# Cosine-weighted linear attention and a Swish MLP on one core: transposes by DMA and attention matmuls in 64-wide array tiles

## The chip, the core and the metric

The kernel runs on one core of a Trainium2 chip. The metric is the device time in microseconds of one execution. Beside it stand the span of a profiled execution (from its first to its last instruction) and the clock that TensorE was granted, as a share of the full clock.

## What is computed

Eight batches, eight heads, 576 positions, 64 features per head. In the attention, q and k pass a relu and are weighted by the cosine and the sine of their position, which doubles the features to 128; v is summed against k once per head, and every query reads that sum. The rows are then fed to an MLP of width 512 to 2048 to 512 with g = h * sigmoid(beta h).

```python
q_p = phi(q, cos_w, sin_w)          # relu(q)*cos, relu(q)*sin
k_p = phi(k, cos_w, sin_w)
kv = np.einsum('bhsf,bhsd->bhfd', k_p, v)
z = np.sum(k_p, axis=2)
num = np.einsum('bhsf,bhfd->bhsd', q_p, kv)
den = np.einsum('bhsf,bhf->bhs', q_p, z)[..., None] + 1e-06
attn_out = num / den
x = attn_out.transpose(0, 2, 1, 3).reshape(B * S, H * D)     # 4608 x 512
h = x @ w_in
g = h * (1.0 / (1.0 + np.exp(-beta * h)))
return g @ w_out
```

## The kernel before

**Layout.** A batch's position is 9p + n, with p from 0 to 63 and n from 0 to 8. `raw_q`, `raw_k` and `raw_v` hold a batch in fp32: partition (g, p) with g the parity of the head, then four head pairs' members j, then n and the features. So one partition half holds the even heads and the other the odd ones.

**Attention of a batch.** `q_relu` and `k_relu` write `qb` and `rk` in bf16. `v_scale` writes v times the cosine and times the sine into `vb`, whose 65th column holds the weight itself, so that one product gives the sum over k too. `q_transpose` turns q on TensorE, 18 blocks of 128x128 in three groups u, and takes each group out of PSUM twice: `rt_c` is a copy, `rt_s` a product with the tangent (since sin = cos * tan, the common cosine falls out in the division and only meets the epsilon, in `epsc`). `kv_mm` is, for each half jp of the heads, 18 matmuls of 64x128 weights and 260 moving columns; `kv_mask` multiplies them by a block mask into `kv`, because 128 weight columns hold two heads and only the diagonal blocks are wanted. `num(b, ci)` takes 128 positions (64 in the last of five groups): 8 matmuls of 128x128 weights and 130 columns, then `den`, `rden` and `x_sb`. `x_transpose` turns the four 128x128 blocks of `x_sb` on TensorE and copies them to `xt`.

**MLP.** The 4608 rows go in nine chunks c of 512. A chunk has 32 slots: slots 0 to 15 are `h_group(c, jt)`, four matmuls of 512 columns into one of two `h_ps` banks and the activation `g_t` on ACT; slots 16 to 31 are `o_part`, four matmuls each into `o_ps`; after every fourth part ACT copies `o_sb`, and two DMAs store it.

**Order.** It is written by hand (a manual schedule). Chunk c carries the attention of batch c+1: `att_units` lists the pieces with the slot after which each is issued, q's transposes after slots 3, 5 and 7, `kv` after 12 and 14, `num` after 16 to 24, x's transposes after 19 to 27. Batch 0 stands before chunk 0 (its last group in slots 3 and 5), batch 1 in chunk 0 by the table `early` and in a tail behind it. So chunks 1 to 6 have attention beside the MLP; chunks 7 and 8 have none. Loads all go by SP's queue, `load_batch(c + 2)` at the head of a chunk's code; stores by POOL's queue to chunk 5, then by SP's. DMAs that share a queue issue in order, and an engine's instruction waits behind those in front of it.

Of the kernel before, what the change touches and what calls it, by code (L numbers as in the profile page):

```python
# [16 lines left out]
P = 128  # L17
# [5 lines left out]
def kernel(  # L23
# [11 lines left out]

    nc = tc.nc
# [9 lines left out]
    NCI = 5  # L46
    MCI = [128, 128, 128, 128, 64]
# [21 lines left out]
    def raw_view(src, b):  # L69
        return src[b].rearrange("(j g) (p n) d -> (g p) j (n d)", g=2, n=NQ)  # L70

    def load_raw(b, name, src, parts=1):
        t = raw_pool.tile([P, 4, NQ, D], FP32, name=f"raw_{name}", tag=f"raw_{name}")
        raws[name, b] = t
        w = 4 // parts
        for i in range(parts):
            nc.sync.dma_start(
                out=t[:, i * w : (i + 1) * w].rearrange("q j n d -> q j (n d)"),
                in_=raw_view(src, b)[:, i * w : (i + 1) * w, :],
            )  # L80
# [20 lines left out]
    w_in_v = moe_w_in.rearrange("(mi p) f -> p mi f", p=P)  # L101
# [3 lines left out]
    def load_w(kind, i):  # L105
        st = stage.tile([P, 4, 512], FP32, name="w_stage", tag="w_stage")
        src = w_in_v[:, :, i * 512 : (i + 1) * 512] if kind == "in" else w_out_v[:, 4 * i : 4 * i + 4, :]
        nc.sync.dma_start(out=st, in_=src)
        stages[kind, i] = st

    def cast_w(kind, i, eng="dve"):
        st = stages.pop((kind, i))
        if kind == "in" and eng == "act":
            nc.scalar.copy(win[i], st)
        elif kind == "in":
            nc.vector.tensor_copy(win[i], st)
        else:
            for jj in range(4):
                j = 4 * i + jj
                nc.vector.tensor_scalar(wout[i][:, jj, :], st[:, jj, :],  # L120
                                        scalar1=rbeta[:, j : j + 1], scalar2=None, op0=ALU.mult)
# [406 lines left out]
```

## Time and profile before

| what | value |
|---|---|
| three runs | 356.45, 356.62, 359.05 us; median 356.62 |
| the profiled execution | 358.02 us, its span 356.3 us |
| granted TensorE clock, mean | 0.961 |
| instructions | 5161, of which 2048 matmuls |
| HBM read, written | 36.71 MB, 9.44 MB |
| first `h_ps` matmul | 34.41 us |
| chunk 0, chunk 1 | 43.59 us, 37.96 us |
| each of chunks 2 to 6 | 35.68 us |
| chunk 7 | 28.38 us |

A timeline row has its start, its length, the engine, the line, the operation with what it writes and reads, and the count of merged instructions; the bracket says how long the engine was idle just before and who ended that. A group row has after the bar the busy time, the mean in ns of one, and the idle time before them. PE is TensorE's matmuls and PEld its weight loads; SPq, ACTq and POOLq are DMA issues. Matmuls overlap in the pipeline: their pace is read from start to start, not from the length of one.

### The profile page before, as it was taken

What the parts mean: (1) busy time and instruction counts of PE and PEld (TensorE: products, weight loads), DVE (VectorE), ACT (ScalarE), POOL (GpSimd) and SP (SyncE); (2) the same over time, 40 slices, a digit from 0 to 9 for tenths busy, and PEclk for the clock granted to TensorE, in tenths of its full rate; (3) what the DMA queues carried; (4) which work ended last, traced back from release to release, by engine and by line L of the source; (5) the groups of instructions that cost most, each with busy time, mean ns of one, the idle gap of its engine ahead of it and who ended that gap; (6) DMA issues with size and microseconds to landing.
All of it is one profiled execution on the core that took longest, in us unless ns stands there. A gap on an engine that the chain in (4) does not pass through costs nothing.

```text
span 356.3 us, 5161 instructions
## 1 busy us (share of the span) xinstructions
PE 328.2 (92%) x2048; PEld 166.1 (47%) x2085; DVE 168.6 (47%) x443; ACT 135.3 (38%) x204; POOL 34.3 (10%) x66
## 2 busy tenths in 40 slices
PE   4665999869999999999999999999999999999994
PEld 2344444434454446444544454445444544444441
DVE  3267492987546554655565556555655530000000
ACT  6334560105511661166116611661166116615711
POOL 3400000220012101210121012101210000000000
PEclk9865899978999999999999999999999999999999
DMA  7953999854712571257125712201220121022022
GB/s 268 393 210 122 362 390 383 307 222 138 262 29 54 175 262 29 50 177 262 29 50 178 262 32 46 45 0 31 44 46 0 32 59 29 2 59 61 2 57 61
DMA packets 21225, 46.49 MB, mean 130 GB/s; under 512 B 1728, under 2 KB 1744, under 8 KB 21200
## 3 DMA queue, kind: packets, MB, share of 16 engines
q1 hardware_dynamic: 18864, 39.85, 33.0%
q0 software_dynamic: 2304, 6.29, 6.8%
q8 instruction: 16, 0.26, 0.3%
q14 instruction: 9, 0.07, 0.1%
q10 hardware_dynamic: 32, 0.01, 0.0%
HBM read 36.71 MB, written 9.44 MB: 130 GB/s over the span
## 4 chain that ended last, share of the span: by engine, by line
PE 86%; DVE 9%; ACT 2%; issue 1%; ACTq 0%; DVEq 0%
PE h_ps L348 34%; PE o_ps L363 34%; PE num_ps L302 6%; PE kv_ps L276 5%; DVE rt_s L266 3%; PE qt_ps L253 3%; PE xt_ps L327 2%; DVE rt_c L265 2%; PE warm_ps L412 1%; DVE x_sb L315 1%; ACT rt_c L263 1%; DVE vb L231 1%; PE tan_ps L183 1%; DVE wout L120 0%; DVE kv L284 0%
## 5 line engine op out<-in xcount | busy, mean ns | idle before, releaser
L348 PE MATMUL h_ps<-xt,win 128*128 128x512 bf16 x556 | 137.6, 387 | 2.1 <-ACT xt L336 0.7
L363 PE MATMUL o_ps<-wout,g_t 128*128 128x512 bf16 x559 | 134.6, 379 | 1.0 <-issue 0.2
L351 ACT ACTIVATE g_t<-h_ps,beta 128x512 bf16<-128x512 f32 x144 | 99.0, 687 | 66.5 <-PE h_ps L348 66.5
L348 PEld LDWEIGHTS <-win 128*128 128x128 bf16 x576 | 55.2, 99 | 71.0 <-issue 17.1
L363 PEld LDWEIGHTS <-g_t 128*128 128x128 bf16 x576 | 53.0, 98 | 53.5 <-issue 0.4
L373 ACT COPY o_sb<-o_ps 128x512 f32<-128x512 f32 x35 | 20.5, 587 | 128.1 <-PE o_ps L363 124.2
L377 POOL DMA_DIRECT2D out_dram<-o_sb x48 | 27.3, 573 | 219.6 <-ACT o_sb L373 219.5
L266 DVE TENSOR_TENSOR rt_s<-qt_ps,tanr 128x512 bf16<-128x512 bf16 (+1 forms) x48 | 26.2, 546 | 8.6 <-ACT rt_c L263 8.6
L371 DVE COPY o_sb<-o_ps 128x256 f32<-128x256 f32 x1 | 0.4, 423 | 60.5 <-ACT o_sb L370 60.5
L315 DVE TENSOR_TENSOR x_sb<-num_ps,rden 128x512 bf16<-128x512 f32 (+1 forms) x40 | 27.6, 689 | 1.4
L309 DVE TENSOR_SCALAR den<-num_ps,epsc 128x8 f32<-128x8 f32 (+1 forms) x40 | 8.9, 223 | 40.8 <-PE num_ps L302 40.8
L302 PE MATMUL num_ps<-kv,rt_c 128*128 128x130 bf16 (+1 forms) x160 | 24.6, 230 | 3.7 <-DVE x_sb L315 2.6
L284 DVE TENSOR_TENSOR kv<-kv_ps,mask 128x520 bf16<-128x520 f32 x16 | 11.2, 699 | 34.4 <-PE kv_ps L276 34.4
L265 DVE COPY rt_c<-qt_ps 128x512 bf16<-128x512 bf16 (+1 forms) x42 | 14.6, 348 | 21.5 <-PE qt_ps L253 21.5
L302 PE MATMUL num_ps<-kv,rt_s 128*128 128x130 bf16 (+1 forms) x160 | 24.7, 231 | 0.0
L276 PE MATMUL kv_ps<-vb,rk 64*128 64x260 bf16 x288 | 19.8, 279 | 3.1 <-DVE vb L231 3.1
L302 PEld LDWEIGHTS <-rt_c 128*128 128x128 bf16 (+1 forms) x160 | 16.6, 105 | 9.9 <-DVE x_sb L315 3.2
L338 DVE COPY xt<-xt_ps 128x512 bf16<-128x512 bf16 (+1 forms) x40 | 14.2, 363 | 10.3 <-PE xt_ps L327 10.0
L302 PEld LDWEIGHTS <-rt_s 128*128 128x128 bf16 (+1 forms) x160 | 16.7, 104 | 4.4 <-issue 1.5
L276 PEld LDWEIGHTS <-rk 64*128 64x128 bf16 x288 | 13.3, 95 | 11.4 <-issue 5.9
L327 PE MATMUL xt_ps<-ident,x_sb 128*128 128x128 bf16 (+1 forms) x160 | 15.9, 226 | 2.4 <-DVE x_sb L315 2.0
L253 PE MATMUL qt_ps<-ident,qb 128*128 128x128 bf16 x144 | 12.5, 225 | 6.1 <-DVE rt_s L266 6.1
(58 smaller groups left out, 136.1 us busy)
## 6 DMA issues: line engine op xcount, KB each, us to landing
raw_k<-in_k_dram SPq DMA_DIRECT2D x7, 1152.0 KB, 5.3
raw_v<-in_v_dram SPq DMA_DIRECT2D x7, 1152.0 KB, 5.6
raw_q<-in_q_dram SPq DMA_DIRECT2D x7, 1152.0 KB, 6.2
out_dram<-o_sb POOLq DMA_DIRECT2D x48, 128.0 KB, 2.6
w_stage<-in_moe_w_in_dram SPq DMA_DIRECT2D x4, 1024.0 KB, 14.9
w_stage<-in_moe_w_out_dram SPq DMA_DIRECT2D x4, 1024.0 KB, 9.3
out_dram<-o_sb SPq DMA_DIRECT2D x24, 128.0 KB, 2.4
raw_q<-in_q_dram SPq DMA_DIRECT2D x2, 576.0 KB, 4.4
```

The lines of the kernel that those rows point to most:

```text
L253: nc.tensor.matmul(t[:, jp, n - n0, :], lhsT=qb[:, n, 2 * jp : 2 * jp + 2, :], rhs=ident, is_transpose=True, start=(jp == 0 and n == n0), ...
L265: nc.vector.tensor_copy(dst_c, src)
L266: nc.vector.tensor_tensor(dst_s, src, tan_v, op=ALU.mult)
L276: nc.tensor.matmul(t[:, g, 0 : 4 * E], lhsT=rk[hs, n, 2 * jp : 2 * jp + 2, :], rhs=vb[hs, n, :, 2 * jp : 2 * jp + 2, :], start=(n == 0), s ...
L302: nc.tensor.matmul(t[:m, g, jp * 2 * E : (jp + 1) * 2 * E], lhsT=rt[:, g, jp, 2 * ci : 2 * ci + m // half, :], rhs=kv[:, g, jp, cs, :], st ...
L315: nc.vector.tensor_tensor(x_sb[:m].rearrange("q j g e -> q g j e"), nv[:, :, :, 0:D], rden[:m].unsqueeze(3).to_broadcast([m, 2, 4, D]), op ...
L327: nc.tensor.matmul(tv[:, mi, 0:m], lhsT=x_sb[:m, mi], rhs=ident[:m, :m], is_transpose=True, start=(mi == 0), stop=(mi == MI - 1))
L348: nc.tensor.matmul(h_ps, lhsT=win[jt // 4][:, mi, (jt % 4) * P : (jt % 4 + 1) * P], rhs=xt[:, mi, :], start=(mi == 0), stop=(mi == MI - 1))
L351: nc.scalar.activation(g_t, h_ps, AF.Silu, scale=beta[:, jt : jt + 1])
L363: nc.tensor.matmul(o_ps, lhsT=gs[c, jt][:, tt * P : (tt + 1) * P], rhs=wout[jt // 4][:, jt % 4, :], start=(jt == 0), stop=(jt == JT - 1))
L373: nc.scalar.copy(o_sb, o_ps)
L377: eng.dma_start(out=out_v[bb, n], in_=o_sb[hf * half : (hf + 1) * half, :])
```

## The change

**Layout.** Attention now works on nine tokens by head parity throughout: `qb`, `qt`, `qs` and `xs` are partition (g, p), two halves of heads, nine values of n, 128 columns. The mask, `rt_c`, `rt_s` and `epsc` are gone. `kv_mm` computes only the diagonal blocks: for each half 36 matmuls of 64x64 weights and 130 columns, whose four positions are row half g and column half jj. `kv_take` casts the eight blocks of a batch out of PSUM into `kv`, which a memset has zeroed once. `num_mm` has, for three values of n and one half of the heads, 12 matmuls of 128x64 weights and 130 columns into the two partition halves: 72 per batch. `x_div` divides six or twelve head columns of a partition at once. The rows of `w_in` are loaded in the order that this layout gives x, in 20 DMAs on 64 partitions each instead of 4.

**Transposes.** For batches 0 and 1 they stay on TensorE (`q_turn_pe`, `x_turn_pe`), but ACT's copy and DVE's tangent product now take the two banks of a half crosswise. From batch 2 on `q_turn_dma` turns q by one transposing DMA from `qb` to `qt`, POOL makes the tangent product `qs` (`q_tan`), and `x_turn_dma` sends `xs` to `xt` by transposing DMAs, all on SP's queue.

**Queues and order.** The loads of batches 2 to 7 go to ACT's queue, batch 2's at the head of chunk 1 together with batch 3's. Stores stay on POOL's queue to chunk 6. Batch 0 is reordered and divided by half; the first quarter of `w_in` is cast on POOL; batch 1 ends inside chunk 0's slots. PSUM is one tile `ps` of eight banks, assigned by hand.

```diff
+        (eng or nc.sync).dma_start(
+            out=raw_tile(b, name)[:, js].rearrange("q j n d -> q j (n d)"),
+            in_=src.rearrange("(j g) (p n) d -> (g p) j (n d)", g=2, n=NQ)[:, js, :])
...
+    def q_turn_pe(b, jp, bank):
+        parts = ((0, 0, 5), (1, 5, NQ))
...
+        for step in range(2):
+            for e in range(2):
+                i, n0, n1 = parts[e ^ step]
+                if e == 0:
+                    nc.scalar.copy(qt[:, jp, n0:n1], v2[i])
+                else:
+                    tan_mul(nc.vector, qs[:, jp, n0:n1], v2[i], n0, n1)
+
+    def q_turn_dma(b):
+        nc.sync.dma_start(out=qt.rearrange("q s n c -> q (s n) c"),
+                          in_=qb.rearrange("q s n c -> q (s n c)"), transpose=True)
+
+    def q_tan(b, jp):
+        tan_mul(nc.gpsimd, qs[:, jp], qt[:, jp], 0, NQ)
...
     def kv_mm(b, jp):
         for n in range(NQ):
-            for g in range(2):
-                hs = slice(g * half, (g + 1) * half)
-                nc.tensor.matmul(
-                    t[:, g, 0 : 4 * E],
-                    lhsT=rk[hs, n, 2 * jp : 2 * jp + 2, :],
-                    rhs=vb[hs, n, :, 2 * jp : 2 * jp + 2, :],
-                    start=(n == 0), stop=(n == NQ - 1))
+            for jj in range(2):
+                for g in range(2):
+                    hs = slice(g * HP, (g + 1) * HP)
+                    nc.tensor.matmul(
+                        t[jj * HP : (jj + 1) * HP, g], lhsT=rk[hs, n, 2 * jp + jj, :],
+                        rhs=vb[hs, n, 2 * jp + jj].rearrange("q s e -> q (s e)"),
+                        start=(n == 0), stop=(n == NQ - 1))
...
+    def num_mm(b, t, jp, bank):
+        for i in range(3):
+            n = 3 * t + i
+            for cs in range(2):
+                for g in range(2):
+                    gs_ = slice(g * HP, (g + 1) * HP)
+                    nc.tensor.matmul(
+                        ps[gs_, bank, i * 2 * E : (i + 1) * 2 * E],
+                        lhsT=(qt, qs)[cs][:, jp, n, gs_],
+                        rhs=kv[:, g, jp, cs, :],
+                        start=(cs == 0), stop=(cs == 1))
...
+    def x_turn_dma(b, t):
+        for c, o, n0, n1 in pieces(b, t):
+            for jp in range(2):
+                nc.sync.dma_start(out=xt_tile(c)[:, jp, o : o + n1 - n0], in_=xs[:, jp, n0:n1].rearrange("q n c -> q (n c)"),
+                                  transpose=True)
...
     def h_group(c, jt):
-                             rhs=xt[:, mi, :], start=(mi == 0), stop=(mi == MI - 1))
+                             rhs=xt[:, jp, :, g * HP : (g + 1) * HP],
+                             start=(mi == 0), stop=(mi == MI - 1))
...
-            eng = nc.sync if c >= 6 else nc.gpsimd
+            eng = nc.sync if c >= 7 else nc.gpsimd
...
+        21: lambda: (kv_mm(1, 0, 6), kv_mm(1, 1, 6), kv_take(1, 0, 6), kv_take(1, 1, 6)),
+        22: lambda: (q_relu(1, 0), q_relu(1, 1)),
+        23: lambda: cast_w("out", 3),
+        24: lambda: q_turn_pe(1, 0, 4),
+        25: lambda: q_turn_pe(1, 1, 6),
+        27: lambda: (num_mm(1, 0, 0, 4), num_mm(1, 0, 1, 5), x_div(1, 0, (0, 1), 4)),
+        28: lambda: (num_mm(1, 1, 0, 6), num_mm(1, 1, 1, 7), x_div(1, 1, (0, 1), 6)),
+        29: lambda: x_turn_pe(1, 0, (0, 1), 4),
+        30: lambda: (num_mm(1, 2, 0, 5), x_turn_pe(1, 1, (0, 1), 7), num_mm(1, 2, 1, 6)),
+        31: lambda: (x_div(1, 2, (0, 1), 5), x_turn_pe(1, 2, (0, 1), 4)),
...
+            (0, lambda: (q_relu(b, 0), q_relu(b, 1))),
+            (1, lambda: v_scale(b, 0)),
+            (1, lambda: q_turn_dma(b)),
+            (4, lambda: k_relu(b)),
+            (6, lambda: v_scale(b, 1)),
+            (7, lambda: q_tan(b, 0)),
+            (8, lambda: q_tan(b, 1)),
+            (12, lambda: (kv_mm(b, 0, 6), kv_mm(b, 1, 6), kv_take(b, 0, 6), kv_take(b, 1, 6))),
+        ]
+        for t, (slot, bank) in enumerate(((16, 4), (18, 6), (20, 4))):
+            u.append((slot, lambda t=t, bank=bank: (
+                num_mm(b, t, 0, bank), num_mm(b, t, 1, bank + 1), x_div(b, t, (0, 1), bank))))
+            u.append((slot + 1, lambda t=t: x_turn_dma(b, t)))
...
-    load_batch(2)
+    for name in "qvk":
+        load_raw(2, name, eng=nc.scalar)
     for c in range(1, NTC):
         if c + 2 < B:
-            load_batch(c + 2)
+            for name in "qvk":
+                load_raw(c + 2, name, eng=nc.scalar)
```

Three places show how instructions move. The first is ACT between chunk 0 and chunk 1. Before, the activations of chunk 1 follow the copies of chunk 0:

```order
L351 ACTIVATE g_t<-h_ps,beta 128x512 x16
L373 COPY o_sb<-o_ps 128x512 x4
L351 ACTIVATE g_t<-h_ps,beta 128x512 x16
```

In the change, the copies of batch 1's x and six loads stand between them:

```order
L362 COPY o_sb<-ps 128x512
L321 COPY xt<-ps 128x2x128
L321 COPY xt<-ps 128x2x256
L78 DMA raw_q<-in_q_dram 128x4x576
L78 DMA raw_v<-in_v_dram 128x4x576
L78 DMA raw_k<-in_k_dram 128x4x576
L78 DMA raw_q<-in_q_dram 128x4x576
L78 DMA raw_v<-in_v_dram 128x4x576
L78 DMA raw_k<-in_k_dram 128x4x576
L343 ACTIVATE g_t<-ps,beta 128x512 x16
```

So ACT issues loads of two batches ahead of chunk 1's first activation; in chunks 2 to 5 it issues those of one.

The second place is SP from batch 2 on. In the change its queue holds, for batches 2 and 3, the transposes and nothing else:

```order
L241 DMA_TRANSPOSE qt<-qb 128x18x128
L328 DMA_TRANSPOSE xt<-xs 128x3x128 x6
L241 DMA_TRANSPOSE qt<-qb 128x18x128
L328 DMA_TRANSPOSE xt<-xs 128x3x128 x2
L328 DMA_TRANSPOSE xt<-xs 128x2x128 x2
L328 DMA_TRANSPOSE xt<-xs 128x1x128 x2
L328 DMA_TRANSPOSE xt<-xs 128x3x128 x2
```

The loads that stood here have gone to ACT; a group of x that crosses from one chunk's `xt` to the next takes four DMAs instead of two.

The third place is TensorE in chunk 2 after `o_part` of slot 16. Before, a `num` group reads 128 weight columns and its transposes follow later:

```order
L363 MATMUL o_ps<-wout_108,g_t 128x512
L302 LDWEIGHTS rt_c
L302 MATMUL num_ps<-kv,rt_c 128x130
L302 LDWEIGHTS rt_s
L302 MATMUL num_ps<-kv,rt_s 128x130
```

In the change the products for the cosine and for the sine come in pairs, one for each partition half of the output:

```order
L352 MATMUL ps<-wout_89,g_t 128x512
L279 LDWEIGHTS qt
L279 MATMUL ps<-kv,qt 64x130
L279 LDWEIGHTS qt
L279 MATMUL ps<-kv,qt 64x130
L279 LDWEIGHTS qs
L279 MATMUL ps<-kv,qs 64x130
L279 LDWEIGHTS qs
L279 MATMUL ps<-kv,qs 64x130
```

There are 24 such matmuls after slots 16, 18 and 20, and no transpose between this place and the next batch's `kv`.

More of the change, by code (lines that the diff above doesn't have):

```diff
@@ L64 @@
     ctx.enter_context(tc.manual_schedule())
+    ps = psum.tile([P, 8, 512], FP32, name="ps")
     raws = {}
[L69 to L80, printed above, removed]
@@ L400, in load_batch, with warm_pe @@
[L400 to L410 removed]
+            bb, n = divmod((c * TCH + tt * P) // HP + hf, NQ)
+            eng = nc.sync if c >= 7 else nc.gpsimd
+            eng.dma_start(out=out_v[bb, n], in_=o_sb[hf * HP : (hf + 1) * HP, :])
+    def warm_pe(count, w=512, bank=0):
@@ L411, in warm_pe @@
         for i in range(count):
-            nc.tensor.matmul(warm_ps[:, 0:w], lhsT=ident, rhs=zeros[:, 0:w], start=True, stop=True)
-    warm_pe(12)
+            nc.tensor.matmul(ps[:, bank, 0:w], lhsT=zeros[:, 0:P], rhs=zeros[:, 0:w], start=True, stop=True)
+    beta = const.tile([P, JT], FP32, name="beta")
+    rbeta = const.tile([P, JT], FP32, name="rbeta")
     q_relu(0, 0, "act")
-    q_relu(0, 1, "act")
-    q_transpose(0, 0, "act")
-    q_transpose(0, 1, "act")
+    q_relu(0, 1, "dve")
+    for bank, n0, n1 in ((6, 0, 5), (7, 5, NQ)):
+        nc.tensor.matmul(ps[:, bank, 0 : (n1 - n0) * HP], lhsT=ones,
+                         rhs=tdiag[:, n0:n1, :], start=True, stop=True)
```

429 lines of the change are left out of this document (180 added, 249 removed).

## The prediction

> **What bounds the kernel now.** I read the page first, for the engine that is never idle and for the chain that ended last.
>
> ```profile
> PE 328.2 (92%) x2048; PEld 166.1 (47%) x2085; DVE 168.6 (47%) x443; ACT 135.3 (38%) x204; POOL 34.3 (10%) x66
> ...
> PE 86%; DVE 9%; ACT 2%; issue 1%; ACTq 0%; DVEq 0%
> PE h_ps L348 34%; PE o_ps L363 34%; PE num_ps L302 6%; PE kv_ps L276 5%; DVE rt_s L266 3%; PE qt_ps L253 3%; PE xt_ps L327 2%; DVE rt_c L265 2%; PE warm_ps L412 1%; DVE x_sb L315 1%; ACT rt_c L263 1%; DVE vb L231 1%; PE tan_ps L183 1%; DVE wout L120 0%; DVE kv L284 0%
> ```
>
> TensorE carries the chain. The MLP (`h_ps`, `o_ps`) is 68% of the span and isn't changed; what can move is the attention's TensorE work and the waits at the start. Which stage holds how much is read from windows cut at the first `h_ps` matmul of each chunk: startup, chunk 0, chunk 1, two steady chunks, and chunk 7, which holds no attention.
>
> ```profile
> 0.00:34.41 34.41, 20.03 (x124) 12.29 (x124) 15.61 (x39) 15.38 (x24) 6.97 (x18) 0.76 0.69 255
> 34.41:78.00 43.59, 38.68 (x251) 19.47 (x254) 29.67 (x76) 13.34 (x20) 4.33 (x8) 0.93 0.93 342
> 78.00:115.96 37.96, 37.22 (x240) 18.80 (x244) 23.77 (x65) 12.76 (x19) 3.56 (x6) 0.94 0.37 114
> 115.96:151.64 35.68, 35.15 (x240) 18.16 (x243) 20.47 (x57) 13.35 (x20) 4.59 (x8) 1.00 0.41 129
> 187.32:223.00 35.68, 35.16 (x240) 18.14 (x243) 20.47 (x57) 13.35 (x20) 4.60 (x8) 1.00 0.41 130
> 294.36:322.74 28.38, 28.22 (x127) 12.44 (x129) 0.00 (x0) 13.35 (x20) 0.00 (x0) 1.00 0.17 38
> ```
>
> After the stretch come its length, then busy time of PE, weight loads, DVE, ACT and POOL, the granted clock, the DMA share and GB/s. A steady chunk costs 35.68 us and a chunk without attention 28.38, so the attention of one batch costs 7.30 us of TensorE's path there. In startup TensorE is busy 20.0 of 34.4 us and in chunk 0 it idles 4.9: there the waits count as well.
>
> **The change: TensorE in a steady chunk.** These rows price the attention's matmuls.
>
> ```profile
> 119.48 0.61 PE L253 MATMUL qt_ps<-ident,qb 128*128 128x128 bf16 x8
> 119.93 1.89 PE L348 MATMUL h_ps<-xt,win 128*128 128x512 bf16 x7
> 122.13 0.61 PE L253 MATMUL qt_ps<-ident,qb 128*128 128x128 bf16 x8 [0.31 <-DVE rt_s L266]
> ...
> 129.12 1.18 PE L276 MATMUL kv_ps<-vb,rk 64*128 64x260 bf16 x18
> 130.23 1.90 PE L348 MATMUL h_ps<-xt,win 128*128 128x512 bf16 x7
> ...
> 144.59 0.22 PE L302 MATMUL num_ps<-kv,rt_c 128*64 128x130 bf16 x1
> 144.65 0.22 PE L302 MATMUL num_ps<-kv,rt_s 128*64 128x130 bf16 x1
> ```
>
> Start to start, a 128x128 transpose takes 0.056 us (0.45 for eight), one half of `kv` 1.11 us for 18 matmuls (0.062 each), a `num` matmul 0.06. From batch 2 on the change takes away 18 + 20 transposes, 38 x 0.056 = 2.1 us, and the waits around them (0.31 above; a few tenths elsewhere). `kv` becomes 72 matmuls of 64x64 weights and 130 columns, `num` 72 of 128x64 weights instead of 40. Before, `kv` + `num` cost 2 x 1.11 + 40 x 0.06 = 4.6 us.
>
> Whether the small matmuls overlap decides. If none did, 144 x 0.06 = 8.6 us. If four kv tiles and two num tiles ran side by side, 72 x 0.06/4 + 72 x 0.06/2 = 3.2 us. The nearest row to the pace at which pairs of weight load and matmul can be issued at all is the smallest matmul of the trace:
>
> ```profile
> 42.33 0.29 PE L327 MATMUL xt_ps<-ident,x_sb 64*128 64x64 bf16 x4
> ...
> L327 PE MATMUL xt_ps<-ident,x_sb 64*128 64x64 bf16 x32 | 2.4, 198 | 0.7 <-DVE x_sb L315 0.7
> ```
>
> Four of them last 0.29 us with 0.198 for one, so (0.29 - 0.198)/3 = 0.031 us per pair. I take that pace, with the rows of `kv` showing that two row halves do run together (260 columns at 0.062 each, while 130 columns alone take 0.06): 144 x 0.031 = 4.5, plus 0.1 for each of four changes of shape (from the 0.06 between 18 x 0.058 and the 1.11 of a kv half, rounded up), 4.9 us. Bounds 3.4 and 9.0.
>
> The page "TensorEngine Tiling (Array Packing)" of the Trainium skill (Key Properties; Restrictions) says that tiles execute weight loads and matmuls in parallel, but that column tiling switches the fast weight load off. This trace agrees only so far that 128x64 loads keep up with 0.06 us a pair; none runs faster here.
>
> **ScalarE pays for the loads.** The q, k and v loads go from SP's queue to ACT's, three at the head of each of chunks 1 to 5, and batch 2's three stand there too: six ahead of chunk 1's first `g_t`. The prices are SP's rows, each an issue with its duration.
>
> ```profile
> 34.65 0.50 SPq L77 DMA_DIRECT2D raw_k<-in_k_dram  x1
> 35.20 0.50 SPq L77 DMA_DIRECT2D raw_v<-in_v_dram  x1
> 35.80 0.72 SPq L108 DMA_DIRECT2D w_stage<-in_moe_w_out_dram  x1
> 36.56 2.15 SPq L77 DMA_DIRECT2D raw_q<-in_q_dram  x1
> 38.80 1.28 SPq L108 DMA_DIRECT2D w_stage<-in_moe_w_out_dram  x1
> 40.12 5.22 SPq L77 DMA_DIRECT2D raw_q<-in_q_dram  x1
> ...
> 62.93 0.37 SPq L77 DMA_DIRECT2D raw_q<-in_q_dram  x1
> 63.34 0.50 SPq L77 DMA_DIRECT2D raw_k<-in_k_dram  x1
> 63.90 0.50 SPq L77 DMA_DIRECT2D raw_v<-in_v_dram  x1
> ...
> 116.20 0.59 ACT L373 COPY o_sb<-o_ps 128x512 f32<-128x512 f32 x1 [3.19 <-PE o_ps L363]
> 117.02 0.69 ACT L351 ACTIVATE g_t<-h_ps,beta 128x512 bf16<-128x512 f32 x1 [0.23 <-PE h_ps L348]
> ```
>
> Three loads issue in 1.4 us; once about four are under way, an issue lasts as long as a load takes to move, 1.3 to 5.2 us. On SP nothing waited behind. On ACT the first activation does, and TensorE has two `h_ps` banks: it can run two groups without ACT (1.73 us; the row at 119.93 is two groups, 1.89 with the last one's drain). In chunks 2 to 5 the issues start beside the last `o_sb` copy and the first activation slips from 1.06 us after the chunk's start to about 2: 0.9 us lost each (bounds 0, if issuing hides, and 1.4). In chunk 1: four issues of 0.5, then 2.2 and 3.2 make 7.4; less 1.73, plus one activation (0.69), some 6.5, and 2 more for the clock, which the startup row shows at 0.76 where TensorE idles: 8.5 us (bounds 0 and 12).
>
> **What should stay hidden.** The q transpose is one DMA of 18 blocks; the x transposes are 18 blocks in six to eight DMAs, on SP. No row shows a transposing DMA. DVE runs ahead: here are its q relu, 3.2 us ahead of the chunk at 151.64, and the nearest DMAs and POOL work by size.
>
> ```profile
> 148.48 1.35 DVE L215 TENSOR_SCALAR qb<-raw_q 128x2304 bf16<-128x2304 f32 x1
> ...
> raw_q<-in_q_dram SPq DMA_DIRECT2D x2, 576.0 KB, 4.4
> out_dram<-o_sb SPq DMA_DIRECT2D x24, 128.0 KB, 2.4
> ...
> L231 POOL TENSOR_TENSOR vb<-raw_v,sin 128x1152 bf16<-128x1152 f32 x2 | 4.2, 2113 | 6.0 <-DMA raw_v<-in_v_dram 6.0
> ```
>
> By the equal-sized load the q transpose lands in 4.4 us; one block after another at the store's 2.4 us it would be 43. It may take about 15: it starts a little before its chunk, `num` begins some 19 us into it, and POOL's two products (2 x 2.1, at 128x1152) lie between. I take 4.4 to 8 us, hidden, since the bytes are those of that row. x has from slot 19 or 21 to the next chunk, about 10 us. If that cover is gone, the excess is paid in each of six chunks. DVE loses `rt_c`, `rt_s` and `xt` and stays under its 20.5 us a chunk; eight `kv` casts there end before `num`. They cost the sum nothing.
>
> The pages differ: "Advanced Engine Details and Errata" (X-Bar Transpose (TRN2)) of the Trainium skill calls such a DMA as fast as a plain one, while "VectorE: DVE Perf Modes" (The three transpose paths) gives 1309 ns for one 128x128 block. By the second, an estimate for 36 blocks is 47 us a batch, more than a chunk; no run shows which holds.
>
> **Startup and chunk 0.** Here DVE sets the end, by its rows.
>
> ```profile
> L231 DVE TENSOR_TENSOR vb<-raw_v,cos 128x1152 bf16<-128x1152 f32 x2 | 2.7, 1352 | 0.0
> L266 DVE TENSOR_TENSOR rt_s<-qt_ps,tanr 128x512 bf16<-128x512 bf16 (+1 forms) x48 | 26.2, 546 | 8.6 <-ACT rt_c L263 8.6
> L315 DVE TENSOR_TENSOR x_sb<-num_ps,rden 128x512 bf16<-128x512 f32 (+1 forms) x40 | 27.6, 689 | 1.4
> L309 DVE TENSOR_SCALAR den<-num_ps,epsc 128x8 f32<-128x8 f32 (+1 forms) x40 | 8.9, 223 | 40.8 <-PE num_ps L302 40.8
> L312 DVE RECIPROCAL rden<-den 128x8 f32<-128x8 f32 (+1 forms) x40 | 8.1, 202 | 1.4
> ```
>
> Now ACT's copy and DVE's product work on two banks at once, where before DVE waited 8.6 us in all for ACT. The q transposes follow the tan table and, now, two warm-up matmuls instead of twelve:
>
> ```profile
> 4.62 2.28 PE L183 MATMUL tan_ps<-tdiag,ones 64*128 64x320 f32 x4 [4.62 <-DVE tdiag L178]
> ...
> 7.04 4.75 PE L412 MATMUL warm_ps<-zeros,ident 128*128 128x512 bf16 x12
> ```
>
> 6.9 + 2 x 0.4 + 0.3 for beta + 9 transposes at that clock's 0.11 make 9 us. Then DVE has 4 tan products (3.1, at 0.69 per 512 columns), 2 v products (2.7), beta 0.4, 4 casts (0.9), half a k relu (0.7) and 6 divisions of 0.22 + 0.20 + 0.55 (5.8): 13.6; with about 2 of waits for `kv` and `num`, and 1.4 for the last transposes and copy, the first `h_ps` comes at 26 (bounds 24 and 30) instead of 34.4: -8.4. Chunk 0 becomes 28.4 + 4.9 + 36 transposes x 0.056 (2.0) + 2.5 for the last division and copy at its end + 1.7 of other waits = 39.5 (37 to 43) instead of 43.6: -4.1, though batch 0 no longer leaves a rest for it.
>
> **Sum.** Startup -8.4; chunk 0 -4.1; chunk 1 28.4 + 4.9 + 8.5 = 41.8 instead of 38.0, +3.8; chunks 2 to 5 28.4 + 4.9 + 0.9 = 34.2 instead of 35.7, 4 x -1.5; chunk 6 33.3, -2.4; chunks 7 and 8 as before. In all -17.1. The profiled execution took 358.02 us for its span of 356.3; the median of three runs is 356.62, which I start from: 339.5 us.
>
> **Rivals.** (a) *The small matmuls do not overlap*: pairs stay at 0.06 us, 4.1 us more per batch than taken; seven batches lie inside chunks: 339.5 + 28 = 368, slower than before. For it: all 128x64 rows stand 0.06 apart. Against: those all use one column half, and kv's row halves do overlap. It decides from 0.048 us a pair (17.1 lost over 7 x 144). (b) *Transposes late*: from 34.2/36 = 0.95 us a block SP's transposes set the chunk; at 1.2, half of the smallest store, a chunk lasts 43.2, 6 x 9 more: 393. Against: equal bytes land in 4.4 us. The page with 1309 ns speaks for it; by it, as an estimate, 417. (c) *Better than forecast*: ACT's issues cost nothing (-8.5 - 3.6 = -12) or tiles overlap fully (7 x -1.5 = -10): 327 to 329 for one, 317 for both. (d) *The gain is eaten*: ACT's block is 12, chunk 0 43, startup 30, a pair 0.038: 339.5 + 3.5 + 3.5 + 4 + 7 = 358.
>
> **How the numbers follow.** Forecast 0.61, own range 333 to 347; (a) 0.10; (b) 0.07; (c) 0.16; (d) 0.06. The range is 322 to 360: it leaves out (b), most of (a) and the case of both gains in (c). Faster by over 1% (about what a measurement tells from no change): 0.61 + 0.16 + 0.02 of (d) = 0.79; within 1% 0.04 (the rest of (d)), slower 0.17.
>
> **What would show it.** The first `h_ps` near 26; 38 transposes gone from chunks 1 to 6, `kv` + `num` near 5 us there; an ACT gap ahead of chunk 1's first `g_t` with long issues of its own; no TensorE wait on `qs` or `xt`. I am wrong if the steady chunk isn't shorter, or if TensorE waits for a transposing DMA.

## The result, and the profile after

| | before | after |
|---|---|---|
| time, median | 356.53 us (356.23 to 359.05, 4 runs) | 347.28 us (346.01 to 348.06, 4 runs) |
| the profiled execution and its span | 358.02, 356.3 us | 348.06, 346.3 us |
| granted TensorE clock, mean | 0.961 | 0.962 |

The ratio is 0.9722, with an interval of 0.9677 to 0.9767: 2.8% faster, 9 us, where 17 were forecast. Here and below a ratio is to the kernel before, run again beside each kernel, and leaves out the one execution of four that was over 1.5% above the fastest in `b2_loads_on_sp` and in `w_in_half_on_pool`; the medians hold all. The page of after shows first that the work went as said, and then that the chain changed hands.

```profile
PE 306.4 (88%) x2363; PEld 146.2 (42%) x2390; DVE 125.9 (36%) x332; ACT 136.2 (39%) x209; POOL 73.5 (21%) x83
...
PE 68%; DMA 17%; ACTq 5%; DVE 3%; issue 2%; SPq 2%; ACT 1%; POOL 1%; POOLq 0%; DVEq 0%
PE ps L352 32%; PE ps L339 28%; DMA w_stage<-in_moe_w_out_dram 8%; PE ps L279 5%; ACTq L78 5%; DMA qt<-qb 4%; DMA raw_k<-in_k_dram 3%; DMA w_stage<-in_moe_w_in_dram 2%; PE ps L256 2%; SPq L97 1%; DVE wout L114 1%; DVE qs L218 1%; ACT g_t L343 1%; SPq L78 1%; POOL qs L218 1%
```

TensorE is busy 22 us less and DVE 43 us less, but the span fell by only 10. TensorE's share of the chain went from 86% to 68%; DMA, which had none, holds 17%, and ACT's queue of load issues 5%. The windows of after, cut as before at each chunk's first matmul of L339 (the new line of `h_ps`, now a bank of `ps`), say where: startup, then chunks 0 to 7. The columns are those of the windows in the prediction.

```profile
0.00:25.67 25.67, 14.16 (x193) 9.59 (x195) 16.86 (x43) 11.93 (x21) 9.05 (x15) 0.87 0.94 254
25.67:70.07 44.40, 37.47 (x305) 18.56 (x309) 25.96 (x61) 17.86 (x29) 3.92 (x8) 0.96 0.70 221
70.07:112.66 42.59, 34.96 (x270) 16.04 (x272) 21.34 (x59) 13.09 (x20) 9.62 (x9) 0.88 0.74 226
112.66:146.34 33.68, 32.29 (x270) 15.36 (x272) 13.74 (x38) 13.23 (x20) 10.24 (x10) 1.00 0.53 159
146.34:181.35 35.01, 32.30 (x271) 15.35 (x273) 13.73 (x38) 13.23 (x20) 10.25 (x10) 1.00 0.56 163
181.35:218.32 36.97, 33.90 (x270) 15.76 (x272) 13.74 (x38) 13.23 (x20) 10.25 (x10) 0.95 0.68 172
218.32:251.90 33.58, 32.30 (x270) 15.36 (x272) 13.74 (x38) 13.23 (x20) 10.25 (x10) 1.00 0.57 166
251.90:284.38 32.48, 32.22 (x271) 15.38 (x273) 6.40 (x17) 13.34 (x20) 8.91 (x10) 1.00 0.30 67
284.38:312.82 28.44, 28.33 (x128) 12.46 (x129) 0.00 (x0) 13.34 (x20) 1.03 (x2) 1.00 0.15 34
```

Against the forecast (26, 39.5, 41.8, four times 34.2, 33.3): startup and the chunks without loads came out as said or a little better. Chunk 0 is 4.9 us longer and did not shrink at all; chunks 3 and 4 are 0.8 and 2.8 longer. Together with chunk 1 that is the missing 7 us.

**The matmuls.** The timeline of TensorE in chunk 2: the whole of `kv` (L256) and one third of `num` (L279).

```profile
125.87 1.22 PE L256 MATMUL ps<-vb,rk 64*64 64x130 bf16 x72
127.02 2.90 PE L339 MATMUL ps<-xt,win 128*128 128x512 bf16 x12
...
130.71 0.25 PE L279 MATMUL ps<-kv,qt 128*64 128x130 bf16 x2
130.79 0.23 PE L279 MATMUL ps<-kv,qs 128*64 128x130 bf16 x2
...
131.53 1.90 PE L352 MATMUL ps<-wout,g_t 128*128 128x512 bf16 x8
```

72 matmuls of `kv` take 1.15 us from start to the next start, 0.016 each. `num`'s come two at a time, within a group every 0.058 us, 0.029 each. These are the paces of the prediction's lower bound (0.06/4 and 0.06/2). In chunk 6, which has no loads, the attention costs 32.48 - 28.44 = 4.04 us.

**ScalarE's queue.** The waits of TensorE in after are headed by one row: it waits for `g_t` (L343) in five chunks, 14.3 us in all, 6.9 the longest. Here is ACT at the head of chunk 1.

```profile
69.65 0.39 ACTq L78 DMA_DIRECT2D raw_q<-in_q_dram  x1
...
70.16 0.44 ACTq L78 DMA_DIRECT2D raw_v<-in_v_dram  x1
70.72 0.56 ACTq L78 DMA_DIRECT2D raw_k<-in_k_dram  x1
71.37 0.79 ACTq L78 DMA_DIRECT2D raw_q<-in_q_dram  x1
72.19 3.08 ACTq L78 DMA_DIRECT2D raw_v<-in_v_dram  x1
75.31 2.74 ACTq L78 DMA_DIRECT2D raw_k<-in_k_dram  x1
78.09 1.27 ACT L343 ACTIVATE g_t<-ps,beta 128x512 bf16<-128x512 f32 x2 [7.59 <-issue]
```

The first activation stands behind six issues, of which the last two take 3 us each. TensorE's side of it, in the same chunk and in chunk 4:

```profile
70.07 1.89 PE L339 MATMUL ps<-xt,win 128*128 128x512 bf16 x8 [0.46 <-ACT xt L321]
78.83 12.75 PE L339 MATMUL ps<-xt,win 128*128 128x512 bf16 x44 [6.88 <-ACT g_t L343]
...
115.67 10.26 PE L339 MATMUL ps<-xt,win 128*128 128x512 bf16 x44 [1.12 <-ACT g_t L343]
...
186.04 11.87 PE L339 MATMUL ps<-xt,win 128*128 128x512 bf16 x44 [2.81 <-ACT g_t L343]
```

Eight matmuls fill the two banks, then TensorE stands. Read the length too: 44 matmuls take 10.26 us after the short wait, but 12.75 and 11.87 after the long ones. A wait costs a second time, by the lowered clock behind it (0.88 and 0.95 in the windows of these chunks). The wait of 2.44 us in chunk 3 drew none (1.00 there).

Why chunk 4 waits more than chunk 2 stands in ACT's rows there, with SP's transposing DMA of q beside them (two views of the same execution):

```profile
180.53 3.45 SPq L241 DMA_TRANSPOSE qt<-qb  x1
```

```profile
181.67 0.38 ACTq L78 DMA_DIRECT2D raw_q<-in_q_dram  x1
182.14 1.46 ACTq L78 DMA_DIRECT2D raw_v<-in_v_dram  x1
183.64 1.61 ACTq L78 DMA_DIRECT2D raw_k<-in_k_dram  x1
185.30 1.26 ACT L343 ACTIVATE g_t<-ps,beta 128x512 bf16<-128x512 f32 x2 [3.13 <-issue]
```

Three loads alone issue in 1.4 us by the rows of before; beside the transpose, whose issue begins 1.1 us earlier, they take 3.6. In chunk 2, where the transpose is issued 5 us ahead of the loads, no load issue lasts over 0.82 us.

**Chunk 0.** SP issues `w_in` in 20 pieces until 25 us; the tail of its list comes late. SP, then the windows of 6 us in that stretch, then the wait that follows on TensorE:

```profile
4.26 20.77 SPq L97 DMA_DIRECT2D w_stage<-in_moe_w_in_dram  x20
...
27.96 0.37 SPq L78 DMA_DIRECT2D raw_k<-in_k_dram  x1
29.24 3.04 SPq L78 DMA_DIRECT2D raw_v<-in_v_dram  x1
```

```profile
10.00:16.00 6.00, 1.66 (x40) 1.09 (x39) 5.19 (x8) 2.72 (x5) 2.98 (x2) 0.72 1.06 258
16.00:22.00 6.00, 4.75 (x102) 3.67 (x103) 4.31 (x15) 0.84 (x4) 2.37 (x2) 0.71 0.98 204
```

```profile
48.84 3.40 PE L256 MATMUL ps<-vb,rk 64*64 64x130 bf16 x72 [3.51 <-DVE vb L214]
```

Before, the same windows show 397 and 386 GB/s at the same full share of the DMA engines. Behind the wait of 3.51 us `kv` itself takes 3.40 us, in chunk 2 1.22.

### The profile page after: what moved, and what is told of

Same layout as the page of the kernel before. It is cut to its first block, busy times and chain, and to the rows that moved or that the text cites. A ratio compares the mean times of both kernels' runs of the same rounds, so it can differ in the third digit from the quotient of the medians.

```text
span 346.3 us, 5863 instructions
## 1 busy us (share of the span) xinstructions
PE 306.4 (88%) x2363; PEld 146.2 (42%) x2390; DVE 125.9 (36%) x332; ACT 136.2 (39%) x209; POOL 73.5 (21%) x83
## 4 chain that ended last, share of the span: by engine, by line
PE 68%; DMA 17%; ACTq 5%; DVE 3%; issue 2%; SPq 2%; ACT 1%; POOL 1%; POOLq 0%; DVEq 0%
PE ps L352 32%; PE ps L339 28%; DMA w_stage<-in_moe_w_out_dram 8%; PE ps L279 5%; ACTq L78 5%; DMA qt<-qb 4%; DMA raw_k<-in_k_dram 3%; DMA w_stage<-in_moe_w_in_dram 2%; PE ps L256 2%; SPq L97 1%; DVE wout L114 1%; DVE qs L218 1%; ACT g_t L343 1%; SPq L78 1%; POOL qs L218 1%
## 5 line engine op out<-in xcount | busy, mean ns | idle before, releaser
L339 PE MATMUL ps<-xt,win 128*128 128x512 bf16 x576 | 138.4, 387 | 15.4 <-ACT g_t L343 14.3
L352 PE MATMUL ps<-wout,g_t 128*128 128x512 bf16 x550 | 126.4, 380 | 2.5 <-issue 1.6
L343 ACT ACTIVATE g_t<-ps,beta 128x512 bf16<-128x512 f32 x144 | 98.4, 687 | 61.2 <-PE ps L339 47.7
L339 PEld LDWEIGHTS <-win 128*128 128x128 bf16 x576 | 56.3, 99 | 93.4 <-issue 35.9
L362 ACT COPY o_sb<-ps 128x512 f32<-128x512 f32 x35 | 20.5, 586 | 108.8 <-PE ps L352 108.8
L271 DVE CAST kv<-ps 64x130 bf16<-64x130 f32 x60 | 17.5, 292 | 87.8 <-PE ps L256 86.8
L218 POOL TENSOR_TENSOR qs<-qt,tanr 128x1152 bf16<-128x1152 bf16 x12 | 28.3, 2378 | 35.7 <-DMA qt<-qb 26.9
L295 DVE TENSOR_TENSOR xs<-ps,rden 128x768 bf16<-128x768 f32 (+1 forms) x27 | 23.4, 868 | 0.9
L279 PE MATMUL ps<-kv,qt 128*64 128x130 bf16 x288 | 21.2, 229 | 1.3 <-DVE kv L271 1.3
L279 PE MATMUL ps<-kv,qs 128*64 128x130 bf16 x288 | 20.6, 228 | 1.1 <-DVE qs L218 0.6
L279 PEld LDWEIGHTS <-qt 128*64 128x64 bf16 x288 | 16.4, 114 | 11.3 <-issue 10.5
L256 PE MATMUL ps<-vb,rk 64*64 64x130 bf16 x576 | 12.7, 235 | 7.6 <-ACT rk L194 4.0
L214 DVE TENSOR_SCALAR vb<-raw_v,cos 128x256 bf16<-128x256 f32 x63 | 17.1, 348 | 3.4 <-DMA raw_v<-in_v_dram 3.4
L279 PEld LDWEIGHTS <-qs 128*64 128x64 bf16 x288 | 16.7, 113 | 1.4 <-DVE qs L218 0.7
L256 PEld LDWEIGHTS <-rk 64*64 64x64 bf16 x576 | 10.1, 116 | 12.3 <-issue 6.4
```

Of the source, the lines that this page charges most:

```text
L214: nc.vector.tensor_scalar(vb[:, n, :, cs, 0:D], rv[:, :, n, :], scalar1=t[:, n : n + 1], scalar2=None, op0=ALU.mult)
L218: eng.tensor_tensor(dst.rearrange("q n (g p) -> q n g p", g=2), src.rearrange("q n (g p) -> q n g p", g=2), tanr[:, n0:n1].unsqueeze(2).to ...
L256: nc.tensor.matmul(t[jj * HP : (jj + 1) * HP, g], lhsT=rk[hs, n, 2 * jp + jj, :], rhs=vb[hs, n, 2 * jp + jj].rearrange("q s e -> q (s e)") ...
L271: nc.vector.tensor_copy(o, a)
L279: nc.tensor.matmul(ps[gs_, bank, i * 2 * E : (i + 1) * 2 * E], lhsT=(qt, qs)[cs][:, jp, n, gs_], rhs=kv[:, g, jp, cs, :], start=(cs == 0), ...
L295: nc.vector.tensor_tensor(xs[:, jps[0] : jps[-1] + 1, 3 * t : 3 * t + 3].rearrange("q s n (j d) -> q s (n j) d", j=2), nv[:, :, :, :, 0:D] ...
```

## The experiments

Theory A: the missing gain sits in load issues on ACT. Theory C: it sits in the 20 pieces of `w_in`. The rival to both is that transposing DMAs are too slow. Every edit is against the changed kernel.

**1. Loads off ScalarE's queue.** Two kernels: batch 2's three loads alone go back to SP, and all of them do.

```diff
-        load_raw(2, name, eng=nc.scalar)
+        load_raw(2, name)
...
-                load_raw(c + 2, name, eng=nc.scalar)
+                load_raw(c + 2, name)
```

> Batch 2's three loads go back to SP's queue; the later batches' loads stay on ACT's. Theory A (the gain that is missing went into load issues ahead of ACT's activations): TensorE's wait of 6.9 us at the head of chunk 1 and about 1 us of lowered clock behind it go, chunk 1 falls from 42.6 to about 35, the time from 347.3 to 339 or 340. Theory B (chunk 1 is long because batch 2's data come late and its transposes with it): the wait moves to num or to the products on POOL, and the time stays within 2 us of 347.

> All loads of batches 2 to 7 are issued by SP, at the same place of the program, ahead of the next transposes. Theory A: all waits of TensorE for an activation at the chunk heads go (6.9, 1.1, 2.4, 2.8 and 1.0 us by the trace, and the clock lost behind them), chunks 2 to 5 fall to the 32.5 us of chunk 6, and the time to 331 to 334 us. Rival: SP's transposing DMAs now stand behind 1.2 MB loads in one queue, land some 10 us later, and num waits for them: 340 or more, with TensorE waiting for the product on POOL.

Measured: 338.9 us (0.9457 of before, 0.9399 to 0.9516) and 334.12 us (0.9354, 0.933 to 0.9378). The wait for `g_t` falls from 14.3 to 6.6 us with the first edit and is gone with the second. Theory A holds: taking the load issues away from the activations gains 13 us, just short of what it said. But the wait that its rival named shows too, on POOL's product `qs`, in chunk 3 above all. TensorE there:

```profile
151.76 0.25 PE L279 MATMUL ps<-kv,qs 128*64 128x130 bf16 x2 [0.86 <-POOL qs L218]
...
154.09 0.25 PE L279 MATMUL ps<-kv,qs 128*64 128x130 bf16 x2 [1.80 <-POOL qs L218]
...
154.51 3.44 PE L352 MATMUL ps<-wout,g_t 128*128 128x512 bf16 x8
```

2.66 us of waits, and then eight matmuls in 3.44 us instead of 1.90: the chunk takes 37.13 us, the one ahead of it 32.48. SP's row says what is late:

```profile
134.19 11.42 SPq L241 DMA_TRANSPOSE qt<-qb  x1
```

The issue of q's transpose takes 11.42 us; with no loads just ahead of it, it took 5.04 in chunk 1 of the same kernel.

**2. What the transposing DMAs are worth.** First TensorE's transposes for all batches, with loads on ACT as in the change, then the same with all loads on SP.

```diff
-            (1, lambda: q_turn_dma(b)),
+            (3, lambda: q_turn_pe(b, 0, 4, "dve")),
+            (5, lambda: q_turn_pe(b, 1, 6, "dve")),
-            (7, lambda: q_tan(b, 0)),
-            (8, lambda: q_tan(b, 1)),
-            u.append((slot + 1, lambda t=t: x_turn_dma(b, t)))
+            u.append((22 + t, lambda t=t: x_turn_pe(b, t, (0, 1), (6, 7, 4)[t], "dve")))
```

> The transposing DMAs and POOL's products are taken out: batches 2 to 7 turn q and x on TensorE, as batches 0 and 1 do, with the copies on DVE; the 64-wide array tiles stay. Theory: 36 transposes at 0.056 us are 2.0 us, and with the changes between shapes and waits 2.1 to 2.7 us per chunk, in six chunks: 360 to 363 us. Rival 1 (transposing DMAs also lengthen the load issues on ACT, so without them the waits of chunks 3 and 4 fall from 2.6 to 1.1 us): 356 to 358. Rival 2 (the waits for DVE's copies out of PSUM come back): 366 or more, the gain of the change gone.

> All loads of batches 2 to 7 on SP's queue (that alone gave 334.1 us) and, beside it, q and x of these batches turned on TensorE, as batches 0 and 1 are, with DVE taking the results out of PSUM. It prices the transposing DMAs where they delay no load on ScalarE's queue. Theory A: then the DMAs are worth what 36 transposes and their copies cost on TensorE, 36 x 0.056 = 2.0 us and some tenths of waits, 2.1 to 2.5 us in each of six chunks: 347 to 349 us, that is 13 to 15 more than with the DMAs, against 3.6 more where the loads were on ScalarE's queue. Rival B (the transposing DMAs gain little in any case, because the transposes fit into waits of TensorE): 336 to 339 us.

Measured: 350.85 us (0.9829, 0.9802 to 0.9856), only 3.6 above the change, where its theory expected 13 and more and its rival 1 9 to 11; and 339.42 us (0.9484, 0.9455 to 0.9512), 5.3 above its partner by the medians (4.6 by the ratios) instead of 13 to 15.

By the second time alone, rival B seemed to hold: transposing DMAs gain little, because TensorE's transposes fit into waits. The stages say otherwise. Without the DMAs, ACT's issues in chunk 3 last 0.37, 0.47 and 0.52 us again and the wait for `g_t` is 9.7 us instead of 14.3. This is rival 1's mechanism, larger than it was priced. Against a chunk without loads, `pe_transposes` loses 8.6 us in chunk 1 and 0.8 in each of chunks 2 to 5 (42.86 and four times about 35.08, over 34.27), the change 10.1, 1.2, 2.5, 4.5 and 1.1: 7.6 us more beside the transposing DMAs. Of these 6.1 are in chunks 2 to 5; in chunk 1 ACT's issues and the wait for `g_t` are alike (6.88 and 6.83 us), and the wait for `qs` and the clock make the difference.

With loads on SP, every chunk from 1 to 6 takes 34.27 us, while its partner's undisturbed chunks take 32.47: the DMAs save 1.8 us a chunk there, 10.8 in six, but that partner loses 6.0 of it again by the late `qs` of chunks 3 to 5 (4.66, 0.38 and 0.97 over 32.47). So in the change the DMAs take back 7.6 of the 10.8 that they save, most of it by ACT's longer issues.

The next edit follows from that: put the loads on SP behind the transpose of q, so that the transpose runs alone.

```diff
+            units.insert(3, (1, lambda c=c: [load_raw(c + 2, name) for name in "qvk"]))
```

> All loads of batches 2 to 7 on SP's queue, but a batch's three loads stand behind the transposing DMA of q in the chunk instead of ahead of it. Theory D (with the loads ahead, the q transpose shares the DMA engines with 3.4 MB: its issue takes 11.4 us instead of 2.7 to 5, POOL's product comes late, TensorE waits 2.7 us in chunk 3, and its clock is lowered for some us behind the wait): issues of 2.7 to 5 us, no wait for qs, chunks 2 to 5 at 32.5 each, 334.1 - 6 = 328 us, 326 to 330. Rival E (the loads now run into x's transposes or come too late for the next chunk): a wait for xt or for DVE's qb takes its place, 333 to 338 us.

Measured: 328.69 us (0.9191, 0.9167 to 0.9215), in the middle of theory D's range. Chunks 0 to 2 of this kernel, and SP's issue in chunk 3:

```profile
25.47:69.60 44.13, 39.09 (x308) 18.86 (x308) 26.88 (x63) 17.85 (x29) 3.92 (x7) 0.92 0.93 304
69.60:102.07 32.47, 32.47 (x273) 15.35 (x272) 20.04 (x58) 13.19 (x20) 10.15 (x10) 1.00 0.75 187
102.07:134.54 32.47, 32.47 (x273) 15.37 (x272) 13.74 (x38) 13.34 (x20) 10.26 (x10) 1.00 0.55 165
```

```profile
133.08 3.43 SPq L241 DMA_TRANSPOSE qt<-qb  x1
```

TensorE is busy for the whole of every chunk from 1 on, at the full clock; the q transpose issues in 2.7 to 4.1 us and lands in 5.8. This is the best version measured: by the ratios to the kernel before, 5.5% under the change.

**3. Chunk 0 and `w_in`.** In `w_in_plain` the weights are loaded by 4 DMAs on 128 partitions in the order of their rows.

```diff
-                nc.sync.dma_start(
-                    out=st[jj * HP : (jj + 1) * HP, 2 * jp : 2 * jp + 2, f0:f1],
-                    in_=w_in_v[jj, :, jp, :, i * 512 + f0 : i * 512 + f1])
+        nc.sync.dma_start(out=st, in_=w_in_v[:, :, i * 512 : (i + 1) * 512])
```

> w_in is loaded by 4 DMAs on 128 partitions as in the kernel before, with its rows in their own order, so that the first MLP product multiplies other rows than the reference's; its work is the same. Theory C (chunk 0 is 5 us longer than forecast because 20 loads on 64 partitions bring w_in late, to 34 us, and everything behind it on SP): w_in has landed by about 25 us, kv of batch 1 doesn't wait for v any more, chunk 0 falls from 44.4 to about 39.5, the time to 342 or 343. Rival (chunk 0 is bound by the order of batch 1's pieces, by the clock, or by the DMA bandwidth for 15 MB in all): chunk 0 stays above 43 and the time at 346 to 348.

Measured: 340.52 us (0.9527, 0.9466 to 0.9588). Startup 26.15, chunk 0 39.21 instead of 44.40, no wait for `vb`: theory C holds for the place. The time is 6.8 us under the change's, more than theory C said. Of the 6.2 us between the two spans, startup and chunk 0 give 4.7; chunk 4 gives 1.9 (35.03 instead of 36.97), for which `w_in` was loaded long before. Why 20 pieces are slower than 4 was asked by sending half of them to POOL's queue.

```diff
+    load_w_in((0,), nc.sync)
...
+    load_w_in((1,), nc.gpsimd)
```

> Ten of w_in's twenty DMAs on 64 partitions go to POOL's queue, behind its memset; the other ten stay on SP. Loads, queues and everything behind startup as in the change (347.3 us). Theory C1 (the DMAs each wait for the one eight places earlier on SP's queue, so that the tail of SP's list, w_out and the raw k, v and q of batch 1, lands too late for chunk 0): the casts of w_in and the v product of batch 1 no longer wait for DMA, chunk 0 falls from 44.4 to 39 to 40 us, in all 342 to 343 us as with the plain w_in. Theory C2 (a DMA that writes 64 partitions is slow in itself, from whichever queue): the windows of startup move as many GB/s as before the edit (216 to 276), chunk 0 stays at 44, 346 to 348 us.

Measured: 350.2 us (0.9746, 0.9691 to 0.9801), which the intervals can't tell from the change. The profiled execution took 346.2. Chunk 0 fell to 37.61 as C1 asks, but startup grew from 25.67 to 33.67, and the GB/s stayed, as C2 asks. This kernel and then the plain one, from 10 to 16 us (the next 6 us have 252 and 387 GB/s):

```profile
10.00:16.00 6.00, 2.45 (x41) 1.29 (x40) 3.25 (x6) 2.60 (x4) 3.30 (x3) 0.86 1.05 256
```

```profile
10.00:16.00 6.00, 2.58 (x40) 1.25 (x38) 5.44 (x7) 2.51 (x4) 3.44 (x2) 1.00 1.05 396
```

All engines are taken in both, at 250 and at 390 GB/s. So the wait of SP's queue for its own earlier pieces is not the limit: the pieces themselves move slowly. A second queue only lets `w_in` run beside batch 0's v and k (k's median landing 16.1 us instead of 9.0), and startup pays. C1 falls. Joined to loads on SP it is no gain either:

> Both edits together: all loads of batches 2 to 7 on SP's queue, and half of w_in's DMAs on POOL's. Where the two stalls are apart in time (chunk 0 and chunks 1 to 5), their gains add: 334.1 - 4.8 = 329 us, 328 to 331. If the w_in half on POOL brings nothing (C2), 333 to 335. If loads on SP, which stand behind w_in's tail there, take up the same slack, 331 to 333.

Measured: 338.56 us (0.9463, 0.9435 to 0.9491), above the 334.12 with the loads alone; startup 33.23 and chunk 0 37.62, and chunks 3 and 4 at 35.56 and 37.57 by the late `qs`. No forecast of the three fits.

The last pair was to separate partitions from row order: as many pieces, each on 128 partitions.

```diff
+                nc.sync.dma_start(
+                    out=st[:, 2 * jp + g, f0:f1],
+                    in_=w_in_v[jp, g, :, :, i * 512 + f0 : i * 512 + f1])
```

> w_in in as many DMAs of the same size and in the row order of the change, but each of them writes one row block on 128 partitions instead of two blocks on 64; the result is the change's. Theory C2 (a DMA that writes 64 partitions moves w_in at 220 to 280 GB/s, one on 128 at 380 to 400; the half on POOL's queue only moved the wait from chunk 0 to startup): the windows of startup show 330 GB/s instead of 254, startup 26, chunk 0 39 to 40, 340 to 342 us in all. Rival C3 (the gathered row order or the number of DMAs costs it, not the partitions): chunk 0 stays at 44, 346 to 348 us.

> Both edits together: loads on SP behind the q transpose, w_in on 128 partitions. If both theories hold, chunk 0 falls from 42.4 to about 39.2 beside it: 328 - 3.2 = 325 us, 322 to 327. If only D holds 328; if only C2 holds 331.

Measured: 411.05 us (1.1522, 1.1473 to 1.1571) and 393.63 us (1.1005, 1.0977 to 1.1033), outside every expectation; chunk 0 takes 109 and 110 us. From 30 to 80 us of the first:

```profile
30.00:80.00 50.00, 11.95 (x30) 3.97 (x31) 2.45 (x2) 4.63 (x7) 1.04 (x1) 0.54 0.13 50
```

A DMA share of 0.13 is two engines of sixteen: the source's outermost dimension, `jj`, has two entries. The edit changed more than the partitions, so it does not answer its question. The page "DMA: Bandwidth & Descriptors" of the Trainium skill (Why a DMA increments its semaphore by 16 and not by 1) says that a DMA's engines are the largest number up to 16 that divides the slowest dimension of both sides; by that rule two engines, as measured here.

What stays open is why the change's own pieces, whose outermost dimension is 64, move 204 to 258 GB/s with all engines busy. The packet records of the traces narrow it. From 16 to 22 us a packet of 2048 bytes takes 156 ns in the change (median) and 88 ns in `w_in_plain`; from 30 to 60 us of `w_in_128_partitions` it takes 84 ns, with pieces as small and rows gathered as in the change. So neither small pieces nor gathered rows make a packet slow by themselves, which leaves the 64 partitions. That is argued, not shown, because there two engines were at work and not sixteen.

**4. Do the array tiles overlap?** Two kernels: `num` with six matmuls into one column half and then six into the other; `kv` with two of its four tiles.

```diff
-        for i in range(3):
-            n = 3 * t + i
-            for cs in range(2):
-                for g in range(2):
+        for g in range(2):
+            for i in range(3):
+                n = 3 * t + i
+                for cs in range(2):
```

> num's twelve matmuls of a group are issued six into one column half, then six into the other, instead of by turns; the arithmetic is the same. Theory O (the low bound of a pair of 128x64 weights and 130 columns, about 0.030 us, comes from two column halves of the array working at once): each matmul alone takes 0.058 to 0.062 us, the 72 of a batch 2.1 us longer, in seven batches that lie inside chunks or beside chunk 0 about 15 us: 361 to 363 us. Rival P (0.030 us is the pace at which pairs are issued, and the halves do not matter): 346 to 348 us.

```diff
-                    hs = slice(g * HP, (g + 1) * HP)
+                    hs = slice(0, HP)
```

> All 72 kv matmuls of a batch read their weights and data from partitions 0 to 63, so that two of the four 64x64 tiles are used (it sums the even heads twice and leaves the odd ones out). Theory T (a matmul of 130 columns holds its tile for 0.058 us, and the pace of 0.016 us comes from four tiles at once): two tiles make 72 x 0.058 / 2 = 2.1 us instead of 1.15, 0.95 more in each of seven or eight batches: 353 to 356 us. Rival P (0.016 us is the pace at which pairs are issued, whatever the tiles): 346 to 348 us.

Measured: 347.72 us (0.9716, 0.9676 to 0.9757) and 352.17 us (0.9846, 0.98 to 0.9892). `num` in the first, chunk 2:

```profile
130.63 0.24 PE L279 MATMUL ps<-kv,qt 128*64 128x130 bf16 x1
130.71 0.22 PE L279 MATMUL ps<-kv,qs 128*64 128x130 bf16 x1
130.77 0.25 PE L279 MATMUL ps<-kv,qt 128*64 128x130 bf16 x2
...
131.29 0.25 PE L279 MATMUL ps<-kv,qs 128*64 128x130 bf16 x2
131.38 0.22 PE L279 MATMUL ps<-kv,qt 128*64 128x130 bf16 x1
```

and `kv` in the second:

```profile
126.52 2.23 PE L256 MATMUL ps<-vb,rk 64*64 64x130 bf16 x72
```

Theory O's number failed, by its premise. Two matmuls run alone, then they come in pairs. The rows don't name the half; but within one half `qt` and `qs` alternate, so two of a kind together are of different halves. Then the seventh, the first of the other half, starts beside the third, and the halves overlap without being issued by turns. The time alone would have spoken for rival P; the rows show one half at 0.06 us a matmul and two halves at two per 0.06. Chunk 6, which has no loads, takes 32.89 us instead of 32.48 for the matmuls that run alone.

`kv` decides it the other way round: with half the tiles it takes 2.23 us instead of 1.22, as theory T says (2.1 instead of 1.15). Chunk 6 takes 33.49 us instead of 32.48, so a batch pays 1.0. The whole time is 0.8 us under T's range: batches 0 and 1 do not pay it in full (startup and chunk 0 end at 70.49 instead of 70.07), and the four runs lie 4 us apart. So the pace is set by tiles that run side by side.

## Why the prediction was right or wrong

- **Startup**, 26 us: right, 25.67. The working by DVE's rows held.
- **Chunk 0**, 39.5 (37 to 43): wrong, 44.40. The failed step is the sum there: it has no term for `w_in` in 20 pieces, though that edit was known, and the windows of before show the DMA engines full at 397 and 386 GB/s just there, with nothing to spare. "1.7 of other waits" left out what the plain load shows as 5.2 us of this chunk, chiefly the wait for `vb` and the slow `kv` behind it.
- **The small matmuls**, 4.9 us a batch: right that the tiles overlap, sized too high. The pace of 0.031, taken from four transposes of 64 columns whose weights all lie in one row half, was thought to bound the issue of any pair; it measured 0.016 for `kv` and 0.029 for `num`. That makes 3.2 us, and 0.8 for the changes of shape instead of 0.4: 4.04 in all. Rival (a), from 0.048 on, is out.
- **ScalarE at chunk 1**, 8.5 us: right for the issues. `pe_transposes`, with no transposing DMA, lost 8.6. The change lost 42.59 - 32.48 = 10.1, of it 6.88 wait (6.5 said), 2.5 lowered clock over 44 matmuls (2 said), 0.5 for `qs`. The issues of about 3 us came as SP's rows had them.
- **ScalarE in chunks 2 to 5**, 0.9 each: right for the issues, which cost 0.8 each in `pe_transposes`, but too low in two chunks of the change. Against 32.48 they lost 1.2, 2.5, 4.5 and 1.1. The step priced the issues by SP's rows in chunk 0 of before, where no transposing DMA ran; close behind one they stretch from 0.5 to 1.0 to 1.6 us, and chunk 4's wait drew the lowered clock.
- **Transposes hidden**: right for TensorE, wrong for the sum. They land in 7.2 us (median; 4.4 to 8 taken), but the one of chunk 1, behind six loads, takes 15.4, and TensorE waits 0.5 us for `qs` there: the prediction's own sign of being wrong, at its smallest. The failed step is "I take 4.4 to 8 us, hidden", for which the sum has no term: a hidden transfer still delays others' issues. Chunks 1 to 5 lose 7.6 us beside these DMAs, 6.1 of them in chunks 2 to 5, by ACT's longer issues and the clock behind the waits. The q transpose also misses the 4.4 us of the load of equal bytes, and an issue of 11.4 us beside loads shows that its price hangs on what runs with it. So this trace doesn't bear out that such a DMA is as fast as a plain one, as "Advanced Engine Details and Errata" (X-Bar Transpose (TRN2)) of the Trainium skill has it. It is far, too, from 1309 ns a block, the figure of "VectorE: DVE Perf Modes" (The three transpose paths) of the Trainium skill: 7.2 us for 18 blocks are 0.4 each.
- **The rivals**: (d), the gain eaten, came in two of its four terms, chunk 0 and ACT; (b) asks for 0.95 us a block, and 0.4 was measured; (c) held for the tiles, at 7 x 0.86 = 6 us instead of 10. With ACT's issues taken away too (12), chunk 0's 4.6 is added back, and 339.5 - 6 - 12 + 4.6 = 326 stands beside the 328.7 measured.

In sum: chunk 0 +4.9; chunks 1 to 5 beside the transposing DMAs +7.6; the attention of six chunks 6 x -0.8 = -4.9; ACT's issues themselves and startup -0.6. These are the 7 us between the 17 forecast and the 10 of the spans. The time lies in the stated range of 322 to 360 us, just above the forecast's own 333 to 347. That two misses of 12.5 us together did not carry it further is luck: matmuls cheaper than taken covered 4.9 of them.

## What to carry to other kernels

A DMA issue is an instruction of the engine that issues it: put loads on a queue where nothing that matters stands behind, and count how many are under way, because issues beyond the first few last as long as transfers (the fifth and sixth here 3.08 and 2.74 us). When two kinds of transfer share the engines, order them by who is waited for: the transpose first, the prefetch behind it, gained 5.4 us with no work removed. And when an edit moves the total little, cut the span into stages before judging it: the time alone of two kernels here spoke for the wrong rival (transposes on TensorE with the loads on SP, and `num` by halves), and their rows did not.

## What the runs showed that was not expected

- A DMA whose source has an outermost dimension of 2 ran on two of sixteen engines, 50 GB/s, and cost 64 us.
- `w_in` in pieces of 64 partitions moved 204 to 258 GB/s with every engine busy, from one queue or two, against 386 to 397 in whole DMAs on 128. A packet of 2048 bytes took 156 ns instead of 88; the cause is not shown.
- A transposing DMA and plain loads stretch each other: its issue 2.7 to 11.4 us, theirs 0.5 to 1.6.
- TensorE started matmuls of the second column half ahead of earlier issued ones of the first, as the pairs of like names have it.
- 2.7 us of waits within 4 us drew 3.44 us of matmuls at nearly half pace.
